# Eight fewer load transfers in a two-round attention and MLP decode kernel

## The chip, the cores and the metric

The kernel runs on one core of one Trainium2 chip. What counts is the device time of one execution in microseconds (us). Before the change three runs gave 711.56, 711.78 and 711.82 us, median 711.78.

The engines are named as the profile names them: PE (TensorE), DVE (VectorE), ACT (ScalarE), POOL (GpSimd) and SP (SyncE). SP computes nothing here; it issues the transfers (DMAs) from device memory into the core's own memory.

## The reference

Two layers are applied, and then applied again with the same weights: attention of one new token over a window of cached keys and values, and an MLP with ReLU. All of it is float32.

```python
x = x + attention(layernorm(x), k_cache, v_cache, wq, wo)   # 4 batches, 32 heads of 128, window 1024
x = x + relu(layernorm(x) @ w1) @ w2                        # 640 -> 1728 -> 640
x = x + attention(layernorm(x), k_cache, v_cache, wq, wo)
x = x + relu(layernorm(x) @ w1) @ w2
```

In the attention `q = x @ wq`, the scores of a head are q times the last 1024 keys, scaled and put through a softmax, the values are summed with these weights, and all heads together are multiplied with `wo`.

## The kernel before, in words

**Layout.** Everything that belongs to a head lies in one record of 9472 float32 columns on 128 partitions: 640 columns of `wq`, 4096 of keys, 4096 of values and 640 of `wo` (lines 47 to 48: `WQ, K, V, WO`, `REC`). A column here is 4 bytes on each of 128 partitions, 512 bytes. The records of all heads follow one another in `rec`, and `wm` holds the MLP's weights, 8640 columns of w1 and 8640 of w2. The data is larger than the core's memory and is read once in each round, except for what five heads keep.

**Places.** The tile `store` has a short front piece and five slots of a record each; `home(h, r)` (line 180) says which slot a head has. `ring` is a small buffer for the MLP's weights of round one, `kept` holds parts of head 26. Heads 27 to 31 are the last of round one and the first of round two, so their keys and values stay in place.

**The list of loads.** Lines 186 to 277 write the whole list of transfers, in order, into `items`. `load` (193) appends one; `run` (204) cuts a stretch of `rec` into the parts of its heads; `piece` (209) takes a part of one head; `group` (213) loads several heads in unequal transfers whose sizes `GROUPS` (82 to 85) gives; `ending` (219) loads the last three heads of a round in halves and, in round one, the six late `wo` parts (225 to 229), since these are used only after the last head. `W1_SLOT` (77) joins the five blocks of w1 of round two into transfers.

**What sets the order.** `pump` (279) issues the next item on SP when nothing that is still in use overlaps its destination (`live`); PE's steps call `done`, which frees places and pumps again. SP takes its instructions in order. A transfer also waits for the one eight places back in SP's list, whose semaphore it uses again. All other engines' instructions are recorded by one helper, so that in the profile of before nearly everything has line 102.

**Attention.** Heads are pipelined (513 to 538): in each step PE computes the scores of head n+1, the weighted values of head n, the query of head n+2, and then the transposed output of head n and its projection by `wo`. The softmax between them is on DVE and ACT. In the profile a PE row `misc<-xT,store` is a query (10 matmuls), `sc_ps<-store,qT` scores (16), `o_ps<-store,scratch` values (16), `t_ps<-rows,scratch` the transposed output, and `acc<-store,oTs` the projection. A row `acc<-kept,small` or `sc_ps<-kept,small` is one of the `busy` fillers (351), which compute nothing that is used.

**MLP.** `mlp` (460): the blocks of w1 in turn (`sc_ps<-ring,xT` or `sc_ps<-store,xT`), two transposes and the ReLU on DVE, then the tiles of w2 (`acc<-store,scratch`), two matmuls each. In round two w1 lies in the slot of head 22 and w2 in that of head 23, w2 in transfers of 22, 20, 8 and 4 tiles (3520, 3200, 1280 and 640 columns). A last copy on DVE and one transfer bring the result out.

Of the kernel before, what the change touches and what calls it, by code (L numbers as in the profile page):

```python
# [39 lines left out]
B, D, H, DH, W, FF = 4, 640, 32, 128, 1024, 1728  # L40
# [6 lines left out]
WQ, K, V, WO = 0, D, D + 4 * W, D + 8 * W  # L47
REC = 2 * D + 8 * W
# [28 lines left out]
W1_SLOT = [[0, 1], [2, 3], [4]]  # L77
# [5 lines left out]
LAST_FIVE = [REC + 4736, 2 * REC - 4736, REC, REC]  # L83
THREE = [REC + HALF, REC + HALF]
GROUPS = [{h: FIVE for h in range(0, 25, 5)}, {6: THREE, 9: FIVE, 14: FIVE, 19: LAST_FIVE}]
# [24 lines left out]
def decode_kernel(ctx: ExitStack, tc: tile.TileContext, xf, rec, wm, out):  # L110
# [82 lines left out]
    def load(src, lo, hi, buf, col, parts):  # L193
        items.append((src[:, lo:hi], buf, col, hi - lo, parts))
# [14 lines left out]
    def piece(r, h, lo, hi, buf="store", col=None):  # L209
        run(r, h * REC + lo, h * REC + hi, buf, home(h, r) + lo if col is None else col)  # L210
# [8 lines left out]
    def ending(r, hs, late):  # L219
        a, b, c = hs[-3:]  # L220
        end = WO if late else REC
        for h, lo, hi in ((a, 0, V), (b, 0, V), (a, V, end), (c, 0, V), (b, V, end), (c, V, WO if late else KEPT)):
            piece(r, h, lo, hi)
        if late:
            for h in hs[-1:] + hs[-LATE:-1]:
                if h == LAST - 1:
                    piece(r, h, WO, REC, "kept", WO - KEPT)
                else:
                    piece(r, h, WO, REC)
# [3 lines left out]
    for h in hs[:-3]:  # L233
        if h in GROUPS[0]:
            group(0, h, GROUPS[0][h])
        if h >= 25:
            piece(0, h, 0, KEPT if h == LAST - 1 else WO if h >= H - LATE else REC)
        if h == LAST - 1:
            piece(0, h, KEPT, WO, "kept", 0)
# [10 lines left out]
    for lo, hi, buf, col in IN_RING:  # L250
        piece(1, new[0], lo, hi, *place(buf, col))
    places = [("store", old[i] + lo, old[j] + hi) for i, lo, j, hi in (
        (0, 0, 0, K), (0, K + 1024, 0, K + VH), (0, K + VH + 1536, 0, V), (1, 0, 1, K), (1, K, 1, K + VH), (1, K + VH, 1, V),
# [25 lines left out]
    def pump():  # L279

        while items:
            src, buf, col, n, parts = items[0]
            if any(b == buf and x < col + n and col < y for b, x, y in live):
                return
            sp.dma_start(buffers[buf][:, col:col + n], src)
            live.append((buf, col, col + n))
            for key, lo, hi, c in parts:
                at.setdefault(key, []).append((lo, hi, buf, c))
            items.pop(0)
# [313 lines left out]
```

## Time and profile before

| what | value |
|---|---|
| median of 3 runs | 711.78 us |
| the profiled execution | 712.25 us |
| its span, first to last instruction of the program | 710.5 us |
| read from device memory | 301.34 MB, 424 GB/s over the span |
| time of the packets of SP's queue | 98.9% of 16 DMA engines' span |
| PE / DVE / ACT busy | 72% / 41% / 14% of the span |
| mean granted clock of PE | 0.803 |
| transfers | 87 from SP, 1 from ACT |

The profile has one execution. A row of an engine gives its start in us from the span's start, its length, the engine, the line, the operation with what it writes and reads, and in square brackets the idle time ahead of it with what ended it. Durations and the sum of the prediction are against the profiled execution; its span is 1.75 us shorter than its time, and its time 0.47 us above the median.

### The profile page before, as it was taken

Reading aid. Unit: us, or ns where it says so; the run is one execution under the profiler, and the core shown is the slowest. Engines: PE = TensorE matmul, PEld = TensorE weight load, DVE = VectorE, ACT = ScalarE, POOL = GpSimd, SP = SyncE. Lnnn points to the kernel's source line nnn. Section 1 sums busy time; section 2 is a strip of 40 time slices with the busy share of each in tenths; the row PEclk is TensorE's granted clock in tenths of the full one; section 3 lists DMA queues with packets and bytes.
Section 4 is the critical chain, followed back from the end, with each engine's and each line's share of the span. In section 5 each row is a group of like instructions: output and inputs, shape, how many; then the busy total and the mean of one; then the engine's idle time right before and its main releaser. Section 6 shows DMA issues by size and latency. Waiting matters only on the chain.

```text
span 710.5 us, 8480 instructions
## 1 busy us (share of the span) xinstructions
PE 513.0 (72%) x3722; PEld 214.0 (30%) x3722; DVE 293.3 (41%) x518; ACT 99.7 (14%) x210; POOL 1.1 (0%) x9
## 2 busy tenths in 40 slices
PE   0777586677584578869888999656584678686986
PEld 0332232232331223333323443222241232332322
DVE  3242353243342343435531775525162243453651
ACT  0110110011010110111120422101010011011110
POOL 0000000000000000000000000000000000000000
PEclk9977787677778776877999999968597677777989
DMA  9999999999999999999999999999999999999996
GB/s 398 439 416 447 425 435 443 414 439 450 418 435 441 424 437 421 423 439 423 430 398 403 412 426 433 445 435 437 431 435 426 438 436 430 432 432 416 433 425 281
DMA packets 12596, 301.96 MB, mean 425 GB/s; under 512 B 1408, under 2 KB 1552, under 8 KB 4624
## 3 DMA queue, kind: packets, MB, share of 16 engines
q1 hardware_dynamic: 12528, 301.42, 98.9%
q8 instruction: 29, 0.48, 0.2%
q14 instruction: 7, 0.06, 0.0%
q10 hardware_dynamic: 32, 0.01, 0.0%
HBM read 301.34 MB, written 0.08 MB: 424 GB/s over the span
## 4 chain that ended last, share of the span: by engine, by line
DMA 72%; PE 23%; DVE 4%; issue 1%; ACT 1%; ACTq 0%; SPq 0%; DVEq 0%
DMA store<-rec 65%; PE sc_ps L102 9%; PE o_ps L102 6%; DMA store<-wm 4%; PE acc L102 3%; PE misc L102 3%; DMA ring<-wm 2%; DVE scratch L102 2%; PE t_ps L102 1%; DVE o_ps L102 1%; ACT oTs L102 1%; DVE small L102 0%; DVE sc_ps L102 0%; ACT sc_ps L102 0%; ACTq L102 0%
## 5 line engine op out<-in xcount | busy, mean ns | idle before, releaser
L102 PE MATMUL sc_ps<-store,qT 128*32 128x512 f32 x1024 | 194.5, 849 | 35.7 <-DMA store<-rec 34.3
L102 PE MATMUL misc<-xT,store 128*128 128x4 f32 x620 | 95.6, 281 | 109.8 <-DMA store<-rec 109.8
L102 DVE TENSOR_REDUCE small<-sc_ps 128x1 f32<-128x1024 f32 x64 | 78.4, 1224 | 181.3 <-PE sc_ps L102 181.2
L102 PE MATMUL o_ps<-store,scratch 128*16 128x512 f32 x960 | 149.5, 701 | 1.7 <-DMA store<-rec 1.4
L102 PEld LDWEIGHTS misc<-xT,store 128*128 128x128 f32 x620 | 90.2, 227 | 166.6 <-DMA store<-rec 119.4
L102 ACT ACTIVATE sc_ps<-sc_ps,small 128x1024 f32<-128x1024 f32 x64 | 69.8, 1091 | 322.6 <-DVE small L102 322.6
L102 DVE STREAM_TRANSPOSE sc_ps<-sc_ps 128x1024 f32<-128x1024 f32 (+1 forms) x70 | 80.8, 1155 | 0.1
L102 PEld LDWEIGHTS sc_ps<-store,qT 128*32 128x32 f32 x1024 | 41.5, 139 | 112.4 <-issue 60.7
L102 PEld LDWEIGHTS o_ps<-store,scratch 128*16 128x16 f32 x960 | 33.8, 117 | 117.4 <-issue 107.8
L102 DVE TENSOR_TENSOR o_ps<-o_ps,of_block 128x512 f32<-128x512 f32 x62 | 43.3, 699 | 50.6 <-PE o_ps L102 50.6
L102 DVE TENSOR_TENSOR qT<-misc,rows 128x4 f32<-128x4 f32 x61 | 9.5, 155 | 112.9 <-PE misc L102 112.9
L102 PE MATMUL acc<-store,oTs 128*4 128x160 f32 x488 | 34.1, 363 | 17.0 <-ACT oTs L102 17.0
L102 DVE TENSOR_REDUCE scratch<-o_ps 128x128 f32<-128x512 f32 x62 | 42.9, 691 | 2.1
L102 ACT COPY oTs<-t_ps 128x4 f32<-128x4 f32 x59 | 9.6, 163 | 207.4 <-PE t_ps L102 207.4
L102 PE MATMUL t_ps<-rows,scratch 128*128 128x4 f32 x118 | 25.8, 289 | 11.3 <-DVE scratch L102 10.3
L102 PEld LDWEIGHTS t_ps<-rows,scratch 128*128 128x128 f32 x118 | 21.9, 231 | 17.4 <-DVE scratch L102 13.1
L102 DVE SCALAR_TENSOR_TENSOR scratch<-sc_ps,small,of_batch 128x128 f32<-128x128 f32 (+1 forms) x70 | 23.7, 339 | 3.5 <-PE o_ps L102 0.9
L102 PE MATMUL acc<-kept,small 128*1 128x328 f32 (+2 forms) x54 | 17.7, 433 | 0.0
L102 PEld LDWEIGHTS acc<-store,oTs 128*4 128x4 f32 x488 | 7.1, 84 | 22.5 <-ACT oTs L102 22.1
L102 ACT ACTIVATION_READ_ACCUMULATOR sc_ps<-sc_ps,small 128x1 f32 x64 | 12.3, 193 | 0.0
L102 DVE RECIPROCAL small<-small 128x1 f32<-128x1 f32 x64 | 9.8, 153 | 2.3 <-ACT sc_ps L102 2.3
L102 PE MATMUL acc<-store,scratch 128*4 128x160 f32 x146 | 6.1, 299 | 3.3 <-DMA store<-wm 3.2
(83 smaller groups left out, 99.8 us busy)
## 6 DMA issues: line engine op xcount, KB each, us to landing
store<-rec SPq DMA_DIRECT2D x14, 7872.0 KB, 27.3
store<-rec SPq DMA_DIRECT2D x7, 7936.0 KB, 29.9
store<-rec SPq DMA_DIRECT2D x4, 7104.0 KB, 30.8
store<-rec SPq DMA_DIRECT2D x11, 2368.0 KB, 36.5
store<-rec SPq DMA_DIRECT2D x3, 4736.0 KB, 25.7
store<-rec SPq DMA_DIRECT2D x2, 4416.0 KB, 29.1
store<-rec SPq DMA_DIRECT2D x3, 2048.0 KB, 40.7
store<-rec SPq DMA_DIRECT2D x1, 4160.0 KB, 21.6
```

The costliest lines, as they stand in the source:

```text
L102: r = build(*args, **kwargs)
```

## The change

Eight transfers go; every byte is still loaded, and to the same places.

- Round one's `wo` of heads 27 to 31 come as one transfer with five pieces of 640 columns per partition (`late_outputs`). For that the host writes these five `wo` into `rec` in the order of their slots, and the `wo` of head 26 now goes ahead of them.
- Head 25 and the front of head 26 are one transfer of 9472 + 6784 = 16256 columns.
- In round two, the two halves of 2048 columns between `K` and `V` of one place are one transfer of 4096.
- Round two's last group of five heads comes as 15744, 15872 and 15744 columns (`FIVE`) for 14208, 14208, 9472 and 9472 (`LAST_FIVE`).
- Round two's w1 comes as three and two blocks, where it came as two, two and one.

```diff
-W1_SLOT = [[0, 1], [2, 3], [4]]
+W1_SLOT = [[0, 1, 2], [3, 4]]
...
-LAST_FIVE = [REC + 4736, 2 * REC - 4736, REC, REC]
 THREE = [REC + HALF, REC + HALF]
-GROUPS = [{h: FIVE for h in range(0, 25, 5)}, {6: THREE, 9: FIVE, 14: FIVE, 19: LAST_FIVE}]
+GROUPS = [{h: FIVE for h in range(0, 25, 5)}, {6: THREE, 9: FIVE, 14: FIVE, 19: FIVE}]
...
     def load(src, lo, hi, buf, col, parts):
-        items.append((src[:, lo:hi], buf, col, hi - lo, parts))
+        items.append((src[:, lo:hi], buffers[buf][:, col:col + hi - lo], [(buf, col, col + hi - lo)], parts))
+
+    def late_outputs():
+
+        slots = [(home(h, 0) + WO, home(h, 0) + REC) for h in range(LAST, H)]
+        src = rec.rearrange("p (h c) -> p h c", c=REC)[:, LAST:, WO:]
+        dst = store[:, FIRST:].rearrange("p (h c) -> p h c", c=REC)[:, :, WO:]
+        items.append((src, dst, [("store", a, b) for a, b in slots],
+                      [(("rec", 0, LAST + i), WO, REC, a) for i, (a, _) in enumerate(slots)]))
...
         if late:
-            for h in hs[-1:] + hs[-LATE:-1]:
-                if h == LAST - 1:
-                    piece(r, h, WO, REC, "kept", WO - KEPT)
-                else:
-                    piece(r, h, WO, REC)
+            piece(r, LAST - 1, WO, REC, "kept", WO - KEPT)
+            late_outputs()
...
-        if h >= 25:
-            piece(0, h, 0, KEPT if h == LAST - 1 else WO if h >= H - LATE else REC)
-        if h == LAST - 1:
-            piece(0, h, KEPT, WO, "kept", 0)
+        if h == LAST - 2:
+            run(0, h * REC, h * REC + REC + KEPT, "store", home(h, 0))
+            piece(0, LAST - 1, KEPT, WO, "kept", 0)
+        elif h >= LAST:
+            piece(0, h, 0, WO)
...
-        (0, 0, 0, K), (0, K + 1024, 0, K + VH), (0, K + VH + 1536, 0, V), (1, 0, 1, K), (1, K, 1, K + VH), (1, K + VH, 1, V),
+        (0, 0, 0, K), (0, K + 1024, 0, K + VH), (0, K + VH + 1536, 0, V), (1, 0, 1, K), (1, K, 1, V),
...
-            src, buf, col, n, parts = items[0]
-            if any(b == buf and x < col + n and col < y for b, x, y in live):
+            src, dst, spans, parts = items[0]
+            if any(b == buf and x < hi and lo < y for b, x, y in live for buf, lo, hi in spans):
                 return
-            sp.dma_start(buffers[buf][:, col:col + n], src)
-            live.append((buf, col, col + n))
+            sp.dma_start(dst, src)
+            live.extend(spans)
...
-    rec[:, :, WO:] = np.asarray(A_wo).reshape(H, DH, D)
+    wo = np.asarray(A_wo).reshape(H, DH, D)
+    rec[:, :, WO:] = wo
+    rec[H - NS:, :, WO:] = wo[[next(h for h in range(H - NS, H) if h % NS == i) for i in range(NS)]]
```

The instructions of PE, DVE, ACT and POOL stand in the same order as before; only SP's list differs. Late in round one SP had, for head 25, the front of head 26, and what follows (the first row ends the group of heads 20 to 24):

```order
L102 DMA store<-rec 128x15744
L102 DMA store<-rec 128x9472
L102 DMA store<-rec 128x6784
L102 DMA kept<-rec 128x2048
L102 DMA store<-rec 128x8832 x2
```

and has now:

```order
L101 DMA store<-rec 128x15744
L101 DMA store<-rec 128x16256
L101 DMA kept<-rec 128x2048
L101 DMA store<-rec 128x8832 x2
L101 DMA store<-rec 128x4736 x2
```

The transfers of 9472 and 6784 columns have become one of 16256, ahead of the same rows.

At the end of round one's loads, from the last halves of heads 30 and 31 to the first weights of the MLP, SP had:

```order
L102 DMA store<-rec 128x4736
L102 DMA store<-rec 128x4096 x2
L102 DMA store<-rec 128x640
L102 DMA kept<-rec 128x640
L102 DMA store<-rec 128x640 x4
L102 DMA ring<-wm 128x1728 x2
```

and has now:

```order
L101 DMA store<-rec 128x4736
L101 DMA store<-rec 128x4096 x2
L101 DMA kept<-rec 128x640
L101 DMA store<-rec 128x5x640
L101 DMA ring<-wm 128x1728 x2
```

The part for `kept` moved to the front, and the five for `store` are one row behind it.

In round two, from the last group of five heads (19 to 23) through the halves of heads 24 to 26 to the MLP's weights, SP had:

```order
L102 DMA store<-rec 128x15744
L102 DMA store<-rec 128x14208 x2
L102 DMA store<-rec 128x9472 x2
L102 DMA store<-rec 128x4736 x5
L102 DMA store<-rec 128x2048
L102 DMA store<-wm 128x3456 x2
L102 DMA store<-wm 128x1728
L102 DMA store<-wm 128x3520
L102 DMA store<-wm 128x3200
```

and has now:

```order
L101 DMA store<-rec 128x15744 x2
L101 DMA store<-rec 128x15872
L101 DMA store<-rec 128x15744
L101 DMA store<-rec 128x4736 x5
L101 DMA store<-rec 128x2048
L101 DMA store<-wm 128x5184
L101 DMA store<-wm 128x3456
L101 DMA store<-wm 128x3520
L101 DMA store<-wm 128x3200
```

The first row of 15744 belongs to the group before. The four transfers of heads 19 to 23 are three, and the last of them now reaches from the middle of head 22 to the end of head 23; w1 has one transfer less.

## Rows read from the trace of the kernel before

**Rows 1.** The page: SP's DMA queue, and the chain that ended last.

```profile
q1 hardware_dynamic: 12528, 301.42, 98.9%
...
DMA 72%; PE 23%; DVE 4%; issue 1%; ACT 1%; ACTq 0%; SPq 0%; DVEq 0%
```

**Rows 2.** SP's issues in time, four of round one: start, length.

```profile
344.44 0.33 SPq L102 DMA_DIRECT2D store<-rec  x1
...
350.04 0.33 SPq L102 DMA_DIRECT2D store<-rec  x1
...
359.75 0.33 SPq L102 DMA_DIRECT2D ring<-wm  x1
...
360.53 0.33 SPq L102 DMA_DIRECT2D ring<-wm  x1
```

**Rows 3.** Two stretches: busy time of each engine, PE's clock, DMA share, GB/s.

```profile
360.00:400.00 40.00, 35.15 (x342) 14.10 (x334) 13.82 (x40) 8.51 (x15) 0.00 (x0) 0.96 1.00 396
400.00:420.00 20.00, 18.55 (x175) 8.60 (x178) 13.86 (x22) 4.75 (x11) 0.00 (x0) 1.00 1.02 433
```

**Rows 4.** DMA issues by size: count, KB each, median us from issue to landing.

```profile
store<-rec SPq DMA_DIRECT2D x11, 2368.0 KB, 36.5
...
store<-rec SPq DMA_DIRECT2D x1, 3392.0 KB, 29.2
store<-rec SPq DMA_DIRECT2D x3, 1024.0 KB, 8.1
...
store<-wm SPq DMA_DIRECT2D x1, 1280.0 KB, 6.5
...
out<-scratch SPq DMA_DIRECT2D x1, 80.0 KB, 1.6
```

**Rows 5.** The chain that ended last, in order of time: start, length, what.

```profile
203.84 24.60 DMA store<-rec
...
673.03 31.83 DMA store<-wm
...
704.90 2.83 PE acc L102 x68
```

**Rows 6.** PE in time, end of round one's attention and its MLP.

```profile
363.87 0.74 PE L102 MATMUL acc<-store,oTs 128*4 128x160 f32 x16
...
372.29 1.25 PE L102 MATMUL sc_ps<-store,xT 128*4 128x432 f32 x9 [0.80 <-DMA store<-wm]
```

**Rows 7.** PE in time, round two, behind the last transfer of two groups.

```profile
542.94 1.07 PE L102 MATMUL sc_ps<-store,qT 128*32 128x512 f32 x3 [8.49 <-DMA store<-rec]
...
553.33 2.76 PE L102 MATMUL o_ps<-store,scratch 128*16 128x512 f32 x16
...
599.26 0.96 PE L102 MATMUL sc_ps<-store,qT 128*32 128x512 f32 x3 [2.87 <-DMA store<-rec]
...
609.61 1.93 PE L102 MATMUL o_ps<-store,scratch 128*16 128x512 f32 x16
```

**Rows 8.** PE in time, round two, from head 23's query to the last fillers.

```profile
656.22 1.28 PE L102 MATMUL misc<-xT,store 128*128 128x4 f32 x10 [3.60 <-DMA store<-rec]
...
663.28 1.28 PE L102 MATMUL misc<-xT,store 128*128 128x4 f32 x10
...
678.60 1.28 PE L102 MATMUL misc<-xT,store 128*128 128x4 f32 x10 [0.75 <-DMA store<-rec]
...
684.30 3.61 PE L102 MATMUL o_ps<-store,scratch 128*16 128x512 f32 x16
...
694.12 1.09 PE L102 MATMUL sc_ps<-store,xT 128*4 128x432 f32 x8
...
698.78 1.15 PE L102 MATMUL acc<-kept,small 128*1 128x328 f32 x4
```

**Rows 9.** Two stretches at the end, columns as in rows 3.

```profile
660.86:681.34 20.48, 18.13 (x158) 7.88 (x154) 12.29 (x21) 3.94 (x8) 0.00 (x0) 1.00 1.00 428
681.34:688.16 6.82, 6.39 (x38) 1.48 (x34) 4.14 (x8) 1.37 (x3) 0.00 (x0) 0.50 1.01 429
```

More of the change, by code (lines that the diff above doesn't have):

```diff
@@ L281, in pump @@
         while items:
-            src, buf, col, n, parts = items[0]
-            if any(b == buf and x < col + n and col < y for b, x, y in live):
+            src, dst, spans, parts = items[0]
+            if any(b == buf and x < hi and lo < y for b, x, y in live for buf, lo, hi in spans):
                 return
-            sp.dma_start(buffers[buf][:, col:col + n], src)
-            live.append((buf, col, col + n))
+            sp.dma_start(dst, src)
+            live.extend(spans)
             for key, lo, hi, c in parts:
-                at.setdefault(key, []).append((lo, hi, buf, c))
+                at.setdefault(key, []).append((lo, hi, spans[0][0], c))
             items.pop(0)
```

## The prediction

> **What bounds the kernel now.** I read the page's DMA and chain sections first [rows 1]. One queue carries nearly everything and its packets fill 98.9% of the time of all 16 DMA engines; the chain that ended last is 72% DMA. So the sum of bytes, and whatever each transfer costs beside them, sets the time. Then the queue of SP, where a late `wo` transfer of 640 columns (a column is 4 bytes on 128 partitions, 512 B) is issued the moment an older transfer lands, so that its issue times are landing times [rows 2]. 4736 columns land 5.60 us after their predecessor (344.44 to 350.04), 640 columns 0.78 us after theirs (359.75 to 360.53). That is (5.60 - 0.78) / 4096 = 1.177 ns a column and 0.78 - 640 x 0.001177 = 0.03 us that a transfer costs besides its data.
>
> Last I read the end of the span on PE. The chain waits for the transfer of 3200 columns until 704.86, and from 704.90 PE works 2.83 us through the last tiles of w2, then DVE copies [rows 5]. The transfers behind it are the same 1280 and 640 columns in both kernels. The end is thus the landing of the 3200 columns plus about 5.6 us, as long as PE is ready for it.
>
> **What goes.** SP issues 79 transfers for 87 (ACT's one stays). Four go with the five late `wo`, and one each with: head 25 with the front of head 26, two value-and-key pieces of round two (2048 + 2048), round two's last five heads (three transfers for four), and w1 (two for three). Bytes are the same. By the landings, 8 x 0.03 = 0.24 us. From above: the stretch with most short transfers moves 396 GB/s, the one behind it 433 [rows 3]. If all of that loss, 40 x (1 - 396/433) = 3.4 us over some 24 transfers (landings from 360.5 to 398.9), were a cost by transfer, it would be 0.14 us each, 1.15 us for eight. From below: no row has a transfer with five pieces a partition; the nearest are the single 640-column ones, whose pieces are as long, and whose 0.78 us already holds their packets. So the saving could be nothing. I take 0.2 us, near the direct row.
>
> **Which waits grow.** A joined transfer is issued when the last of its places is free. What covers that is the queue ahead of it: the time from issue to landing, less its own data. A lone transfer on an empty queue (the output) lands 1.6 us after issue, 0.2 of it data, so more than 1.4 us of queue hides an issue completely [rows 4].
> - Head 25 with 26: the 6784 columns of before land 29.2 us after issue with 8.0 of data. 11.1 of the rest is head 25, now in the same transfer; 10 us of queue stay.
> - 2048 + 2048: the median of the three transfers of 1024 KB is the second of this pair, 8.1 us. Less 4.8 of joint data, 3.3 us stay.
> - Groups of five heads as 15744, 15872 and 15744: the shortest issue to landing of one is 24.60 us [rows 5], less 18.5 of data, 6.1 us. The last group now has the pattern of the others.
> - w1: its places come free when head 22's values are done, about 668 below, and its data starts at 692.7 - 6.1 = 686.6 (below); 18 us.
> - Five pieces: a usual SP issue is 0.33 us [rows 2]. Even five of them, 1.7 us, stand behind 10 us of queue.
> So no joined issue leaves the queue dry.
>
> **Which landings come later.** Joining gives up early landings, and that costs where PE is not waiting anyway.
> - Late `wo`. Before, the six land 0.78 us apart from 360.5 to 364.4; now the kept one first and five together at about 364.2. PE projects heads 27 and 28 at 363.87 [rows 6], so this slips by 0.4 us or so. Behind it the MLP begins on weights that have landed, and PE waits 0.80 us for the next at 372.29: covered. The issues that depend on it have at least 3.5 us of queue (1280 KB: 6.5 us less 3.0 of data) [rows 4], 3.0 after the slip, over the 1.4 needed.
> - Head 25 lands 8.0 us later, with the front of head 26. PE's backlog lasts until it catches up with heads 27 to 31, which land at DMA's pace; the halves of heads of 2368 KB that are issued meanwhile are of a kind that lands 36.5 us after its issue (median of eleven in both rounds) [rows 4], 31 of it queue. Nothing.
> - w1: the first joined part lands 10176 columns ahead of the 3200 ones, 704.65 - 12.0 = 692.7, and PE starts on w1 at 694.12 [rows 8]. Nothing.
> - Round two's last group. Before, heads 22 and 23 land separately, PE takes up head 23's query at 656.22 and head 24's at 663.28 [rows 8], 7.1 us later. Now half of head 22's keys, its values and all of head 23 land together at 656.0. This is the pattern of the other groups [rows 7]: PE starts on the rest of the scores at 599.26 and ends the values, ready for the query after next, at 609.61 + 1.93 = 611.54, 12.3 us later. So head 24's query slips by 12.3 - 7.1 = 5.2, less 0.2 for the earlier landing, to 668.3.
>
> That backlog is the one term that can reach the end. Heads 24 to 26 then take the same steps as before at the full clock (1.00 from 660.86 to 681.34 [rows 9]). At 678.60 PE had waited 0.75 us for the last query, so 4.25 us remain. Behind it the granted clock stood at 0.50, the lower level of 1.2 GHz, from 681.34 to 688.16 [rows 9], after that wait and a short query. A PE that comes late has no such wait. At the full level the values of head 25 need 1.93 (as at 609.61) for 3.61 us [rows 7, 8], and 4.25 - 1.7 = 2.55 us remain. The fillers ahead of w2 end at 698.78 + 1.15 = 699.93, so PE is ready at 702.5. The first 22 tiles are 44 matmuls, 1.83 us at the 2.83 for 68 [rows 5], and must be done when the 3200 columns land at 704.65: up to 702.8 nothing is lost. That leaves 0.3 us to spare, little, but on the side of no loss.
>
> **Sum.** Only DMA's saving is left: -0.2 us on a span of 710.5 and an execution of 712.25 us. That execution is 0.47 above the median of the runs, 711.78, so the forecast for the median is 711.6. From about 0.2% (1.4 us) on a difference can be told from none; this is no change.
>
> **Rivals.**
> 1. PE comes too late for w2. It decides from 702.8. If the clock falls at the last query as before, the 4.25 us stay, w2 begins at 704.2, and PE ends 704.2 + 1.83 + 2.83 - 707.73 = 1.1 us later: 712.9. If the group also starts as slowly as at 542.94, ready at 553.33 + 2.76 = 556.09, 13.15 us later [rows 7], 0.9 more: 713.8. I put the case at 713.3. For it: the spare time is 0.3 us and rests on a clock that these rows do not fix. Against: PE was at the full level through all of the stretch that it now reaches without a pause. The Trainium skill (DMA: Bandwidth & Descriptors, "Why a DMA increments its semaphore by 16 and not by 1") says that only the full count means that all data has landed; by it head 22 gets nothing from the joined transfer early, the trace agrees (the scores resume only at 599.26), and this rival cannot be softened by early rows.
> 2. Transfers cost the 0.14 us of the bound from above: -1.15 us, 710.6. For it the low rate in [rows 3]; against it the 0.03 of [rows 2].
> 3. A transfer holds the engines for the 1.4 us that the lone output needs beside its data [rows 4]: eight of them, 11 us, 700.6. Against it, landings 0.78 us apart with 0.75 of data [rows 2]. The Trainium skill (the same page, "Anatomy of one DMA") gives a fixed cost near 2.0 us a transfer, and its "Rules for kernel authors" ask to coalesce; taken as engine time that would be 16 us. The trace disagrees: it lies beside other transfers.
> 4. The MLP's short transfers start late: the 0.4 us slip is three or more, the 3.5 us of queue runs out, and 1 to 3 us are lost: 713.5.
>
> **How the numbers follow.** Forecast 0.63, rivals 0.22, 0.10, 0.01 and 0.04. Below 710.4 lie rival 3 and a fifth of rival 2: faster 0.03. Above 713.2 lie half of rival 1 and a part of rival 4: slower 0.12. Same 0.85. The range goes from rival 2's 710.6 to 713.2, with about 0.06 left out below and 0.12 above.
>
> **What would show it.** Right: DMA busy throughout; the 3200 columns land 0.1 to 0.4 us earlier; PE idle for some us ahead of 656 and then busy without a pause past 680; a short wait for the 3200 columns still there near 704.5. Wrong: no wait of PE for w2, and the last tiles begin after 705 (rival 1); 396 GB/s from 360 to 400 well up (rival 2); gaps between packets there (rival 4).

## The result: slower, by about 1.5 us

The changed kernel takes **713.32 us** (median of 19 runs, 712.06 to 715.51), the kernel before **711.78 us** (median of 19 runs in the same comparison, 710.93 to 713.58). The ratio is **1.0021, 95% interval 1.0012 to 1.0031**: slower, though by little, and 0.1 us beyond the upper end of the predicted range. The profiled execution took 713.34 us with a span of 711.6, where before it was 712.25 and 710.5.

### The profile after

The page of the changed kernel: packets of the whole span, SP's queue, and the chain that ended last, which answer to [rows 1].

```profile
DMA packets 11956, 301.96 MB, mean 424 GB/s; under 512 B 1280, under 2 KB 1424, under 8 KB 4368
...
q1 hardware_dynamic: 11888, 301.42, 98.9%
...
DMA 63%; PE 29%; DVE 5%; ACT 1%; issue 1%; another core or an unknown queue 1%; ACTq 0%; SPq 0%; DVEq 0%
```

The same bytes go in 640 packets fewer (12528 on this queue before, 11888 now), at the same share of the 16 engines. So DMA still carries the kernel, and joining bought nothing that could be seen: had the transfers' own cost held the queue back, the mean rate should have risen, and it went from 425 to 424 GB/s.

Windows of the changed kernel, with the columns of [rows 3] (the last three are PE's granted clock, DMA's share, GB/s): the stretch with the short transfers, and the one behind it.

```profile
360.00:400.00 40.00, 34.94 (x341) 13.91 (x334) 13.44 (x37) 8.45 (x15) 0.00 (x0) 0.96 0.99 386
400.00:420.00 20.00, 18.54 (x168) 8.33 (x170) 13.87 (x25) 4.80 (x12) 0.00 (x0) 1.00 1.01 430
```

386 GB/s for 396: over 40 us that is 0.4 MB, or 0.9 us at the 430 of the row below. The execution's span is 1.1 us longer. Here, then, nearly all of it is lost, in the end of round one's attention and in its MLP.

PE's timeline of the changed kernel, for the end of round one's attention and the MLP's first blocks (start, length, and at the end the idle time before and what ended it).

```profile
364.49 0.73 PE L101 MATMUL acc<-store,oTs 128*4 128x160 f32 x16 [0.44 <-DMA store<-rec]
...
367.67 1.04 PE L101 MATMUL sc_ps<-ring,xT 128*4 128x432 f32 x8
...
372.33 1.25 PE L101 MATMUL sc_ps<-store,xT 128*4 128x432 f32 x9 [0.23 <-DMA store<-wm]
...
374.75 0.91 PE L101 MATMUL sc_ps<-ring,xT 128*4 128x432 f32 x8 [0.81 <-DMA ring<-wm]
```

The same place in the kernel before (rows not shown ahead; the values of head 31 first).

```profile
359.87 3.06 PE L102 MATMUL sc_ps<-store,scratch 128*16 128x512 f32 x16 [2.45 <-DVE scratch L102]
...
367.06 1.04 PE L102 MATMUL sc_ps<-ring,xT 128*4 128x432 f32 x8
...
374.35 0.91 PE L102 MATMUL sc_ps<-ring,xT 128*4 128x432 f32 x8 [0.45 <-DMA ring<-wm]
```

The projection of heads 27 and 28 now waits for a transfer, 0.62 us later than the 363.87 of [rows 6], and the MLP's first block starts 0.61 us later. The transfer that PE next waits for lands when it did (372.33, for 372.29 in [rows 6]), but the one behind it, the first that reuses the ring, lands 0.4 us later. SP's timeline says why. The first columns of the ring are free when PE's first block of the MLP has read them; only then is their reload issued. Before:

```profile
368.18 3.13 SPq L102 DMA_DIRECT2D ring<-wm  x3
```

and in the changed kernel:

```profile
368.79 3.13 SPq L101 DMA_DIRECT2D ring<-wm  x3
```

The last transfer ahead of the reload is the one of 2160 columns (1080 KB) that was issued at 364.30; on the page of before it is

```profile
store<-wm SPq DMA_DIRECT2D x1, 1080.0 KB, 7.9
```

so it lands at 372.2 (372.24 by the trace). Thus 4.06 us of queue stood before this reload, and now 3.5. I call this number the queue ahead of the reload; it is the number that decides, as the experiments show.

At the end, PE's timeline of the changed kernel, answering to [rows 7, 8].

```profile
657.20 1.07 PE L101 MATMUL sc_ps<-store,qT 128*32 128x512 f32 x3 [6.86 <-DMA store<-rec]
...
669.48 1.28 PE L101 MATMUL misc<-xT,store 128*128 128x4 f32 x10
...
703.80 1.15 PE L101 MATMUL acc<-kept,small 128*1 128x328 f32 x4
704.75 4.00 PE L101 MATMUL acc<-store,scratch 128*4 128x160 f32 x112
```

and its clock where [rows 9] had 1.00:

```profile
660.86:681.34 20.48, 18.52 (x146) 8.07 (x144) 11.57 (x20) 3.68 (x9) 0.00 (x0) 0.83 1.00 429
```

The last group of five behaves as forecast: one long wait, then a backlog, with head 24's query 12.3 us behind the first scores. PE reaches w2 at 704.75 and runs its 112 matmuls without a wait, where before 68 of them stood behind the landing of the 3200 columns [rows 5]. So PE, not a landing, now ends the chain, which looks like rival 1. But PE was hardly late: the 3200 columns, issued at 674.88 and 30.9 us under way,

```profile
store<-wm SPq DMA_DIRECT2D x1, 1600.0 KB, 30.9
```

landed at 705.80, 0.94 us later than before (704.86), and PE ended w2 2.95 us behind that landing, where before it needed 2.83. So of the 1.1 us by which this span is longer, 0.94 are a later landing and 0.1 PE. The experiments e1 and e4 below say the same.

### The profile page after: what moved, and what is told of

Same layout as the page of the kernel before. It is cut to its first block, busy times and chain, and to the rows that moved or that the text cites. A ratio compares the mean times of both kernels' runs of the same rounds, so it can differ in the third digit from the quotient of the medians.

```text
span 711.6 us, 8466 instructions
## 1 busy us (share of the span) xinstructions
PE 497.6 (70%) x3722; PEld 209.8 (29%) x3722; DVE 293.0 (41%) x518; ACT 99.6 (14%) x210; POOL 1.1 (0%) x9
## 2 busy tenths in 40 slices
DMA packets 11956, 301.96 MB, mean 424 GB/s; under 512 B 1280, under 2 KB 1424, under 8 KB 4368
## 3 DMA queue, kind: packets, MB, share of 16 engines
q1 hardware_dynamic: 11888, 301.42, 98.9%
## 4 chain that ended last, share of the span: by engine, by line
DMA 63%; PE 29%; DVE 5%; ACT 1%; issue 1%; another core or an unknown queue 1%; ACTq 0%; SPq 0%; DVEq 0%
DMA store<-rec 61%; PE sc_ps L101 12%; PE o_ps L101 8%; PE acc L101 5%; PE misc L101 3%; DVE scratch L101 2%; DVE o_ps L101 2%; DMA ring<-wm 2%; PE t_ps L101 2%; ACT oTs L101 1%; DVE small L101 0%; ACT sc_ps L101 0%; DVE sc_ps L101 0%; ACTq L101 0%
## 5 line engine op out<-in xcount | busy, mean ns | idle before, releaser
L101 PE MATMUL sc_ps<-store,qT 128*32 128x512 f32 x1024 | 190.0, 829 | 45.6 <-DMA store<-rec 44.3
L101 PE MATMUL misc<-xT,store 128*128 128x4 f32 x620 | 93.8, 278 | 115.6 <-DMA store<-rec 115.6
L101 PE MATMUL o_ps<-store,scratch 128*16 128x512 f32 x960 | 142.8, 664 | 3.8 <-DVE small L101 1.4
L101 PEld LDWEIGHTS misc<-xT,store 128*128 128x128 f32 x620 | 88.4, 223 | 171.0 <-DMA store<-rec 123.5
L101 PEld LDWEIGHTS o_ps<-store,scratch 128*16 128x16 f32 x960 | 32.0, 112 | 111.9 <-issue 100.8
L101 ACT ACTIVATION_READ_ACCUMULATOR sc_ps<-sc_ps,small 128x1 f32 x64 | 12.3, 193 | 0.0
```

The source lines that it names most:

```text
L101: r = build(*args, **kwargs)
```

## The experiments

Four theories are named in the expectations:
- **T**: the last group of five makes PE late for w2 (rival 1).
- **W** (in some texts M): the five late `wo` come in one landing, PE starts the MLP late, the ring's reload is issued late, and DMA runs dry (rival 4).
- **P**: a transfer of several pieces a partition disturbs the DMA engines by itself.
- **C**: PE's wait for the five pieces makes the granted clock fall, and PE's slowness costs, whatever the DMA does.

Each was timed in five rounds against the kernel before on the same chip, whose median was 711.83 to 712.13 us in those comparisons. The last three columns are of its profiled execution: the reload's issue, and GB/s in the windows 364 to 372 and 364 to 400 us. Behind 400 us all of them move 431 to 433 GB/s until 680, and counted in bytes no profiled execution regains or adds more than 0.3 us between 400 and 680. What an execution gains or loses behind 680 the table doesn't show; e9 and e16 below lost 1 to 2 us there.

| | median us (runs) | ratio, 95% interval | reload | 364:372 | 364:400 |
|---|---|---|---|---|---|
| before | 711.78 (19) | | 368.18 | 385 | 392 |
| changed | 713.32 (19) | 1.0021 (1.0012 to 1.0031) | 368.79 | 368 | 382 |
| e1 | 715.54 (6) | 1.0045 (1.0032 to 1.0057) | 370.13 | 320 | 371 |
| e2 | 713.01 (11) | 1.0017 (1.0008 to 1.0025) | 368.73 | 369 | 381 |
| e3 | 712.30 (11) | 1.0003 (0.9994 to 1.0012) | 367.62 | 397 | 390 |
| e4 | 711.71 (11) | 1.0000 (0.9991 to 1.0009) | 367.65 | 397 | 401 |
| e5 | 714.49 (5) | 1.0038 (1.0025 to 1.0051) | 370.58 | 326 | 370 |
| e6 | 712.60 (11) | 1.0011 (1.0002 to 1.0020) | 368.72 | 382 | 393 |
| e7 | 711.70 (12) | 0.9999 (0.9990 to 1.0009) | 367.69 | 394 | 396 |
| e8 | 712.38 (12) | 1.0018 (1.0004 to 1.0033) | 370.92 | 313 | 357 |
| e9 | 713.25 (12) | 1.0015 (1.0003 to 1.0027) | 368.54 | 378 | 380 |
| e10 | 711.95 (12) | 1.0000 (0.9988 to 1.0012) | 367.54 | 397 | 403 |
| e11 | 713.03 (12) | 1.0016 (1.0007 to 1.0026) | 370.35 | 324 | 365 |
| e12 | 713.92 (12) | 1.0022 (1.0013 to 1.0032) | 369.88 | 336 | 367 |
| e13 | 712.38 (11) | 1.0005 (0.9996 to 1.0014) | 368.11 | 390 | 390 |
| e14 | 712.65 (11) | 0.9998 (0.9982 to 1.0013) | 367.56 | 393 | 400 |
| e15 | 713.64 (11) | 1.0017 (1.0007 to 1.0027) | 367.73 | 396 | 387 |
| e16 | 712.28 (11) | 1.0008 (0.9999 to 1.0016) | 367.60 | 397 | 394 |
| e17 | 713.15 (11) | 1.0013 (1.0004 to 1.0022) | 370.18 | 324 | 386 |
| e18 | 715.24 (6) | 1.0053 (1.0041 to 1.0065) | 373.10 | 307 | 353 |

### Which part of the change costs (e1 to e5)

**e1**: the changed kernel, with the last group of five in four transfers again.

```diff
...
-GROUPS = [..., {6: THREE, 9: FIVE, 14: FIVE, 19: FIVE}]
+GROUPS = [..., {6: THREE, 9: FIVE, 14: FIVE, 19: LAST_FIVE}]
```

> The changed kernel, but heads 19 to 23 of round two come in four transfers again (14208, 14208, 9472, 9472). Theory T (PE comes late to the last MLP because heads 22 and 23 land together): the loss goes, 711.5 to 712.0 us (ratio to before 0.9995 to 1.0005), PE waits for w2 twice again, near 701 and 705. Theory M (the joined late wo let the MLP of round one start 0.6 us later and its short loads lose 0.7 to 1 us of DMA time there): 712.3 to 712.9 (1.0008 to 1.0015), the last load lands 0.7 us or more after that of before although PE waits for w2.

**e2**: the changed kernel, with six single late `wo` again.

```diff
-            piece(r, LAST - 1, WO, REC, "kept", WO - KEPT)
-            late_outputs()
+            for h in hs[-1:] + hs[-LATE:-1]:
+                ...
+                    piece(r, h, WO, REC)
...
```

> The changed kernel, but round one's late wo are six transfers again, in the old order; the other joins stay. Theory T: no change from the changed kernel, 712.8 to 713.5 us (1.0015 to 1.0025), no wait of PE for w2. Theory M: 711.9 to 712.6 (1.0003 to 1.0012), the load issued first in the second round of ring buffers (1728 columns) is issued at 368.2 us again and the DMA from 370 to 400 us runs as before.

**e3**: both of these edits. 

> Both undone: six late wo and four transfers for heads 19 to 23; heads 25 and 26, the 4096 columns of round two and w1 stay joined. T and M together, or either: 711.4 to 712.0 us (0.9995 to 1.0003). If one of the three joins that stay costs something, 712.3 or more.

e1 was slower than the changed kernel, not faster: T falls as the cause. Neither theory had its 715.54 us. e3, which keeps heads 25 and 26, the 4096 columns and w1 joined, can't be told from before, though its 712.30 lies a little above what its text expected. e2's 713.01 lies in T's range, not in M's: taking the late `wo` apart alone gave back little. Its profiled execution shows why, there at least. The values of head 31, which took 3.06 us before,

```profile
360.03 3.54 PE L101 MATMUL sc_ps<-store,scratch 128*16 128x512 f32 x16 [2.43 <-DVE scratch L101]
```

ran nearly all at half clock (0.50 from 360.17 to 363.58), and with single late `wo` and no wait for them the reload still came at 368.73, as late as in the changed kernel, with the same 369 and 381 GB/s. So two parts were left, and each was made alone, in the kernel before.

**e4**: `19: LAST_FIVE` becomes `19: FIVE`, and nothing else.

> The kernel of before with only the last group of round two in three transfers (15744, 15872, 15744). Theory T: the whole loss is here, 712.8 to 713.5 us (1.0015 to 1.0025), w2's matmuls run without a wait and begin after 703.7. Theory M: 711.6 to 712.2 (1.000 to 1.0006); PE comes late to w2 by less than it can make up.

**e5**: only the late `wo` are joined, with the code for it.

```diff
-            for h in hs[-1:] + hs[-LATE:-1]:
-                ...
+            piece(r, LAST - 1, WO, REC, "kept", WO - KEPT)
+            late_outputs()
```

> The kernel of before with only round one's late wo joined (kept one first, then five pieces in one transfer); all other loads as before. Theory M (PE waits for the five pieces, begins the MLP of round one some 0.6 us later, issues the ring's next loads later, and the DMA engines run dry there): 712.6 to 713.8 us (1.0012 to 1.0028), gaps of the DMA engines between 364 and 400 us above the 0.8 us of before. Theory T (the last group of five heads): 711.5 to 712.0 (0.9995 to 1.0004).

e5 alone gives 714.49 us, 1.0038, more than its text expected (713.8 at most); e4 gives no loss. Yet in e4 PE is as late for w2 as forecast (its timeline):

```profile
702.20 4.40 PE L102 MATMUL acc<-store,scratch 128*4 128x160 f32 x112
```

It takes up w2 at 702.2 without a wait, inside the 702.8 that the prediction had as its deadline, and no time is lost. In e5 PE waits for the five pieces:

```profile
364.85 0.73 PE L102 MATMUL acc<-store,oTs 128*4 128x160 f32 x16 [1.98 <-DMA store<-rec]
...
369.19 0.60 PE L102 MATMUL sc_ps<-ring,xT 128*4 128x432 f32 x3
```

and SP's first reload of the ring is

```profile
370.58 3.13 SPq L102 DMA_DIRECT2D ring<-wm  x3
```

2.4 us later than before. The wait of 1.98 us is not all of it. The granted clock of e5 falls behind that wait to 0.50, 1.2 GHz:

```profile
365.95:369.36 3.41, 3.41 (x33) 1.60 (x29) 1.05 (x6) 1.42 (x2) 0.00 (x0) 0.50 0.94 392
```

e1 shows the same, 2.01 us of wait and then 0.50 from 365.54:

```profile
364.40 0.73 PE L102 MATMUL acc<-store,oTs 128*4 128x160 f32 x16 [2.01 <-DMA store<-rec]
```

```profile
365.54:368.95 3.41, 3.41 (x33) 1.63 (x29) 1.12 (x6) 1.39 (x2) 0.00 (x0) 0.50 0.94 394
```

The profiled executions of before and of the changed kernel had such a low stretch earlier, before's from 360.49, the changed kernel's from 360.41 (the window 360 to 364 shows 0.57 in both). PE was then late for the late `wo` by itself, and the single landing cost only 0.6 us. In e1 and e5, whose clock is full at 360 us, it costs 2 us of wait, and half speed behind it.

### Lateness without the join (e6, e7), and another order (e8)

**e6** and **e7**: the kernel before, with one and with two fillers ahead of the late projections.

```diff
+        if late > 2:
+            busy()
```

> The kernel of before, all its loads unchanged, with one more filler (two matmuls of 328 columns, 0.6 us) on PE ahead of the late projections of round one. Theory M: the same loss as the joined late wo, 712.4 to 713.8 us (1.001 to 1.0028). Theory P (the transfer of five pieces itself disturbs the DMA engines): 711.6 to 712.1 (0.9998 to 1.0004).

> As the run before it, with two fillers (1.2 us). Theory M: more than with one, 713.0 to 714.8 us (1.0017 to 1.004), longer gaps of the DMA engines from 364 to 400 us. Theory P: 711.6 to 712.3.

e6 slipped as W says and lost 0.1%, though the interval reaches down to 0.02%; its profiled execution moves 382 GB/s up to 372 us but 393 up to 400, no less than before, so the trace doesn't tie that 0.1% to the reload. e7 missed (713.0 to 714.8 us by W, 711.70 measured): its execution had the clock full from 360 to 372 us, PE started on the ring's first weights at 366.73, hardly behind their landing at 366.59 in spite of two fillers, the reload was issued at 367.69, and nothing was lost. That speaks against "later work costs" and for "a later reload costs".

**e8**: the changed kernel, with the five pieces ahead of the kept head and the projections in another order, heads 27 to 31 first.

```diff
-            piece(r, LAST - 1, WO, REC, "kept", WO - KEPT)
             late_outputs()
+            piece(r, LAST - 1, WO, REC, "kept", WO - KEPT)
...
-        for i in range(late - 3) if late > 2 else (0,):
+        for i in (1, 2, 3) if late > 2 else (0,):
...
```

> The changed kernel with all its 80 transfers, but the five pieces are loaded ahead of the part for kept, and PE projects heads 27, 28, 29, then 30, 31 and last 26, so that it does not wait for the five. Theory M: the loss goes or nearly, 711.4 to 712.5 us (0.9994 to 1.001). Theory P or T: as the changed kernel, 712.8 to 713.8 (1.0014 to 1.0028).

The five land sooner, but in the profiled execution PE still waits 1.61 us and its clock falls; the reload comes at 370.92. The median is in M's range, but the runs fall in two groups: eight of 711.7 to 712.6 us and four of 713.8 to 716.5, of which the profiled one (715.17) is one. The ratio is 1.0018, with an interval that holds the changed kernel's 1.0021: a gain isn't shown.

### Clock or reload (e9 to e12)

**e9**: the changed kernel with two fillers in the wait for the five. **e10** and **e11**: the kernel before, and the changed one, with three more fillers behind head 30's values. **e12**: e11 with four fillers in the wait.

```diff
+            if late > 2 and i == 0:
+                busy()
+                busy()
```

```diff
-        values(r, hs[-2], 0, (0, 1))
+        values(r, hs[-2], 0, (0, 1 if r else 4))
```

> The changed kernel with two fillers (1.2 us at the full clock) on PE between the late projection of head 26 and those of heads 27 and 28, where PE waits for the five pieces. Theory C (PE's wait for the five pieces, 0.4 to 2.0 us, lets the granted clock fall to 0.50 at the start of round one's MLP; PE then releases the ring 2 us later and the DMA engines run dry): the clock stays at 1.00 from 364 to 372 us in most executions, 711.6 to 712.6 us (0.9998 to 1.001). Theory P (the transfer of five pieces itself disturbs the DMA engines): as the changed kernel, 712.8 to 713.8.

> The kernel of before with three more fillers (1.8 us) behind the values of head 30 in round one, where PE waits 2.45 us for DVE, so that the clock is at 1.00 when the values of head 31 start. Nothing waits for the late wo here. Theory C: same or a little faster, 710.8 to 711.9 us (0.9986 to 1.0001), clock 1.00 from 360 to 372. Theory P: 711.6 to 712.0.

> The changed kernel with the same three fillers. PE ends the values of head 31 earlier, at 361.7, in every execution, and so waits 2 us for the five pieces in every one. Theory C: slower than the changed kernel though PE is faster, 714 to 716 us (1.003 to 1.006), clock 0.50 from some 365 to 369, the first load of the ring's second round issued near 370.6. Theory P, or a slip of PE alone: as the changed kernel or better, 712.0 to 713.4.

> As the run before it, with four more fillers (2.4 us) in the wait for the five pieces. Theory C: the clock stays at 1.00, PE begins the MLP near 366.8, the ring's load is issued near 368, and most of the loss goes: 711.4 to 712.6 us (0.9995 to 1.001). Theory P: 712.0 to 713.8.

e9 and e12 kept the clock at 1.00 from 360 to 372 us and were no faster for it (1.0015, 1.0022): C alone falls. Their reload was still late (368.54, 369.88). e10 (711.95) equals before. e11 missed its number, 714 to 716 forecast and 713.03 measured, though its reload was as late as it said. e9, e10 and e11 lie in the ranges of P, which e13 and e14 decide, and e12's 713.92 just above P's. In e9's profiled execution, the slowest of its twelve, PE reached w2 only at 706.32 and ended it 3.8 us behind the landing of the 3200 columns (706.51), where before it needed 2.83: there rival 1's lateness cost 1 us.

### One landing or two (e13, e14)

**e14**: the changed kernel, with the five late `wo` in two transfers, three pieces and two, so that heads 27 and 28 land with the first. **e13**: the same in e1.

```diff
+        for a, b in ((2, 5), (0, 2)):
...
+            src = rec.rearrange("p (h c) -> p h c", c=REC)[:, LAST + a:LAST + b, WO:]
+            dst = store[:, FIRST:].rearrange("p (h c) -> p h c", c=REC)[:, a:b, WO:]
...
```

> The slowest kernel so far (changed kernel with heads 19 to 23 in four transfers, 715.5 us) with one thing else: round one's five late wo come in two transfers, three pieces (heads 27 to 29) and two (30, 31), so that PE can project heads 27 and 28 near 362.8 us instead of 364.4. Theory W (PE's wait for the joined late wo makes the first reload of the ring late, and the DMA engines run dry): 711.6 to 712.8 us (0.9997 to 1.0013), reload issued before 368.3. Theory P (transfers with several pieces disturb the DMA engines): 713.5 to 716.

> The changed kernel with the late wo as three and two pieces. Theory W: the part of the loss that the late wo make goes, 711.7 to 713.0 us (0.9998 to 1.0016; the upper end if the last group of five heads with the other joins costs what the run with six late wo showed). Theory P: as the changed kernel or worse, 713.0 to 714.0.

e13 against e1, 1.0005 for 1.0045, and e14 against the changed kernel, 0.9998 for 1.0021, differ in this one cut. Both came out in W's range. A transfer of three pieces a partition is still there, so P falls. e13's difference is clear; e14's is less so, for its interval (0.9982 to 1.0013) reaches that of the changed kernel, and its median is 0.52 us above that of before in the same comparison. In e14 PE has its pieces two us sooner than in e5, and the reload is early:

```profile
362.58 0.73 PE L101 MATMUL acc<-store,oTs 128*4 128x160 f32 x16 [0.44 <-DMA store<-rec]
```

```profile
367.56 3.55 SPq L101 DMA_DIRECT2D ring<-wm  x3
```

### Two that left something open (e15, e16)

**e15**: the changed kernel, with six late `wo` and heads 25 and 26 apart; the last group of five, w1 and the 4096 columns stay joined.

```diff
-        if h == LAST - 2:
-            run(0, h * REC, h * REC + REC + KEPT, "store", home(h, 0))
-        ...
+        if h >= 25:
+            piece(0, h, 0, KEPT if h == LAST - 1 else WO if h >= H - LATE else REC)
...
```

> The run with six late wo (1.0017) with heads 25 and 26 apart again; left of the change are the last group of five in three transfers, w1 in two and the 4096 columns in one. If the joined heads 25 and 26 made that run slow: 711.5 to 712.2 us (0.9995 to 1.0005). If w1 or the 4096 columns with the group of five did, or PE's late arrival at w2: 712.6 to 713.4 (1.001 to 1.002).

1.0017, as e2, and 713.64 us is above what its text expected of either case (713.4 at most). Its profiled execution has an early reload (367.73), so the reload doesn't explain it; e2's has a late one. Why these two kernels are slow in most runs isn't shown.

**e16**: the kernel before, with the place of the first weights released one block later in the program.

```diff
-            done(("w", r), k * FF, k * FF + FF)
+            if r or k:
+                done(("w", r), (k - 1 if k == 1 else k) * FF, k * FF + FF)
```

> The kernel of before, PE's work and all transfers unchanged, but in round one's MLP the place of w1's first block is given free only with the second block, so that the first reload of the ring is issued some 1.5 to 2 us later (near 370). No late wo is joined, PE does not wait for them. Theory W: that alone makes the loss, 713.0 to 715.5 us (1.0017 to 1.005), gaps of the DMA engines between 364 and 402 us of 1.8 us or more (0.8 before). If the lateness of the issue does not matter: 711.6 to 712.2.

The issue did not move (367.60): it waits for PE's last read of the place, wherever the release is written. So e16 is in effect the kernel before once more, and its 1.0008 shows how far apart two such medians may lie. Its profiled execution, 714.34 us, shows a loss that no window ahead of 680 has. PE waited 2.39 us for the first transfer of w2, the granted clock was 0.50 from 702.52 to 709.34, and the last 68 matmuls took 4.67 us where before they took 2.83 [rows 5]:

```profile
705.12 4.67 PE L102 MATMUL acc<-store,scratch 128*4 128x160 f32 x68 [1.33 <-DMA store<-wm]
```

The 3200 columns had landed at 705.08, only 0.2 us later than before. So about 2 us of this execution are PE's clock at the very end, not DMA.

### The reload alone (e17, e18)

In the kernel before, one filler of the MLP reads the first weights instead of kept columns, so that the reload waits for that filler. In **e17** it is the filler behind the second block, in **e18** the one at the end of the third (before, that one stood in the middle of the third), two matmuls behind a landing. Transfers are as before, and so is PE's work, but for the place of one filler in e18.

```diff
...
-                    busy()
-            done(("w", r), k * FF, k * FF + FF)
+                    busy(src=ring if k * FF + FQ * (j + 1) == 3456 else kept)
+            if r or k >= 1:
+                done(("w", r), (0 if k == 1 else k) * FF, k * FF + FF)
```

> The kernel before, all transfers as they were. One filler of round one's MLP (128x328, its result goes into the same unused columns) reads the first weights in the ring instead of kept columns, and the release of those columns is written behind it; so the reload of that part of the ring waits for this filler, and PE's instructions are otherwise the same in number, shape and order. The reload's issue should move from 368.18 to 369.8 to 370.3 us, the queue ahead of it from 4.06 to about 2.2 us. Theory W (the loss of the change is nothing but this late reload: the 16 DMA engines are then partly dry around 371 us and all later loads land later): last load 0.8 to 1.8 us later than in the profile before, median 712.7 to 713.7. Rival C (the loss comes from the clock of PE or from the shape of the joined transfers, the late reload only goes along with it): no change, 711.6 to 712.2, since 2.2 us of queue are more than the 1.4 us that a lone transfer needs.

> As e17, but the filler that reads the first weights stands two matmuls into the third block, which wait for a landing at 372.2 us: the reload is issued at about 372.8 us, some 0.5 us after the transfer ahead of it has landed, so that the queue is surely empty for a while. Theory W: all 16 engines idle from about 372.3 to 373.7 us, most of them longer, 3 to 4 us lost at once, perhaps more where the next reloads come late in their turn: median 714.8 to 718. Rival C: what an empty queue costs is only the gap that can be seen between the landing and the first packets, 1.5 us: 713.2 or below.

Both came out where W had them: 713.15 us (712.7 to 713.7 forecast) and 715.24 (714.8 to 718). e17's median alone proves little, since its interval (1.0004 to 1.0022) overlaps e16's; the trace and e18, whose 1.0053 is clear of everything, carry the argument. PE's MLP starts at 366.99 in e17, as before (367.06); the reload's issue is moved to 370.18, and the two issues behind it follow at 370.60 and 371.09 (369.74 and 370.99 before):

```profile
370.18 1.28 SPq L102 DMA_DIRECT2D ring<-wm  x3
```

This is what it does to the DMA engines. Windows of 1 us, the kernel before (the last two columns are DMA's share and GB/s):

```profile
369.00:370.00 1.00, 1.00 (x11) 0.34 (x5) 0.00 (x0) 0.00 (x0) 0.00 (x0) 1.00 0.93 302
370.00:371.00 1.00, 1.00 (x6) 0.26 (x3) 0.00 (x0) 0.00 (x0) 0.00 (x0) 1.00 0.93 368
371.00:372.00 1.00, 0.49 (x2) 0.00 (x0) 0.00 (x0) 0.00 (x0) 0.00 (x0) 1.00 0.96 403
372.00:373.00 1.00, 0.71 (x8) 0.21 (x10) 0.00 (x0) 0.00 (x0) 0.00 (x0) 1.00 1.07 372
```

e17:

```profile
369.00:370.00 1.00, 1.00 (x12) 0.34 (x6) 0.00 (x0) 0.00 (x0) 0.00 (x0) 1.00 0.62 259
370.00:371.00 1.00, 1.00 (x7) 0.24 (x3) 0.00 (x0) 0.00 (x0) 0.00 (x0) 1.00 0.33 138
371.00:372.00 1.00, 0.43 (x2) 0.00 (x0) 0.00 (x0) 0.00 (x0) 0.00 (x0) 1.00 0.89 185
372.00:373.00 1.00, 0.75 (x10) 0.23 (x12) 0.00 (x0) 0.00 (x0) 0.00 (x0) 1.00 0.96 380
```

e18, whose reload and two next issues come at 373.10, 373.52 and 374.00:

```profile
367.00:368.00 1.00, 1.00 (x12) 0.38 (x4) 0.00 (x0) 0.18 (x1) 0.00 (x0) 1.00 1.08 453
368.00:369.00 1.00, 0.79 (x10) 0.19 (x9) 0.18 (x1) 0.09 (x1) 0.00 (x0) 1.00 0.79 328
369.00:370.00 1.00, 1.00 (x13) 0.27 (x5) 0.00 (x0) 0.00 (x0) 0.00 (x0) 1.00 0.58 245
370.00:371.00 1.00, 0.68 (x4) 0.00 (x0) 0.00 (x0) 0.00 (x0) 0.00 (x0) 1.00 0.37 156
371.00:372.00 1.00, 0.00 (x0) 0.00 (x0) 0.00 (x0) 0.00 (x0) 0.00 (x0) 1.00 0.08 35
372.00:373.00 1.00, 0.85 (x10) 0.46 (x12) 0.00 (x0) 0.00 (x0) 0.00 (x0) 1.00 0.00 0
373.00:374.00 1.00, 1.00 (x9) 0.17 (x2) 0.00 (x0) 0.00 (x0) 0.00 (x0) 1.00 0.00 0
374.00:375.00 1.00, 0.15 (x1) 0.00 (x0) 0.00 (x0) 0.00 (x0) 0.00 (x0) 1.00 0.91 166
```

e18 is the clearest. The transfer ahead lands at 372.1 (PE takes it up at 372.15), so by landings the queue is busy until then. But the share of the engines falls from 368 on: 0.79, 0.58, 0.37, 0.08. The 16 engines don't end their parts of the queue together. The trace has 16 increments of the semaphore for the last transfer ahead, which I read as one for each engine's part: in e18 they come from 368.75 to 372.10, 3.35 us apart, in the kernel before from 368.86 to 372.24. The landing tells only of the last. A reload issued 2 us ahead of that landing (e17) is late for most of them. And behind e18's issue at 373.10 nothing moves before 374.04, 0.94 us. So a reload that is to find no engine idle needs some 3.35 + 0.94 = 4.3 us of queue, an estimate from these two numbers.

## Why the prediction was wrong

**What bounds the kernel**: held in the main. DMA carries the span in every profile, and what the changed kernel and e18 lose they lose as DMA time. From the GB/s of 364 to 400, at 432 GB/s: (392 - 353) x 36 / 432 = 3.3 us for e18, whose span is 3.1 longer, and (392 - 382) x 36 / 432 = 0.8 us for the changed kernel, whose span is 1.1 longer. Not all executions are like that: e16's lost about 2 us to PE's clock in w2 and e9's 1 us to a late PE, behind the last long landing. Such ends are part of the scatter of the medians.

**What goes**: held as far as can be told. Eight transfers fewer are worth nothing that a ratio shows (e3 keeps three of the four single joins, e4 the fourth, and e14 has seven of the eight; 1.0003, 1.0000 and 0.9998). That leaves no room for rival 3. For rival 2 the medians are too coarse, for e14's interval would hold its 0.14 us a transfer; but its sign, a rate well up from 360 to 400, is absent: from 364 to 400 us e14, with seven transfers fewer and an early reload, moves 400 GB/s, and e10, with all of them and as early a reload, 403.

**Which waits grow**: this step failed. The prediction took "more than 1.4 us of queue hides an issue completely" from a lone output, and found 3.5 us of queue, 3.0 behind the slip: covered. So it put the term of the late `wo` at nothing. (Its 3.5 was read from the 1280 KB transfer that is issued at 373.93; the reload that decided, issued at 368.18, isn't in its sum.) The lone output shows what an issue needs when it meets an empty queue. It doesn't show when the queue becomes empty, and landings don't either. By the runs, the stretch from 364 to 372 us moves 393 to 397 GB/s in the seven kernels whose reload is issued by 367.8, 368 to 390 where it comes from 368.1 to 368.8, and 307 to 336 where it comes at 369.9 or later. With the landing ahead at 372.2, some 4.4 us of queue are needed, not 1.4, close to the 4.3 estimated from e18. The changed kernel's 3.5 is already on the slope, and so is before's 4.06 a little.

**Which landings come later**: "slips by 0.4 us or so" is 0.6 in the profiled execution, and in the profiles of e1 and e5 the reload is 2.0 and 2.4 us late. It was read from one execution in which PE happened to be at half clock from 360.49, and so to be late for the late `wo` anyway. Where PE is on time, as in e1 and e5, the one landing makes it wait until 364.4 to 364.9. The Trainium skill (DMA: Bandwidth & Descriptors, "Why a DMA increments its semaphore by 16 and not by 1") says that only the full count tells that the data is there; the traces agree, heads 27 and 28 begin only when all five pieces have landed. The prediction reckoned with that here too ("five together at about 364.2"); what it didn't ask is when PE would be ready for them in an execution at full clock.

**The last group of five**: held. Head 24's query came 12.3 us behind the first scores, as worked out, and in e4 PE was ready for w2 at 702.2 (702.5 predicted). In the changed kernel it was 704.75, 1.2 us of it from the later landing (657.20 for 656.0) and the rest beside a clock of 0.83 where 1.00 was assumed. It cost about 0.1 us, since the 3200 columns came later too. e1 takes this lateness away and gains nothing.

**The rivals**: rival 4 is what happened, and it had 4 chances in 100. That its price fits (713.5; 713.32 measured) is luck: its condition was a slip of "three or more" us, from the wrong 1.4 us, and 0.6 already loses something. Rival 1's sign, no wait for w2, is in the profile too; it cost 0.1 us there and nothing in e4, and 1 us in the profiled execution of e9.

Rival 3's sentence on the Trainium skill (DMA: Bandwidth & Descriptors, "Anatomy of one DMA") leaves out that this section is on transfers issued by gpsimd. SP issues those here, and the rival doesn't rest on that sentence.

**How much is accounted for.** The late reload alone is worth 1.2 us by medians (e17, 713.15 for the 711.97 beside it; its interval is 0.3 to 1.6). e5 has it as late and loses 2.7: there PE is late for the whole MLP, and the next issues slip as well (376.85 for 375.32 in SP's timeline). e17 moves 403 GB/s from 372 to 400, e5 383. In the changed kernel's profiled execution the late reload accounts for the loss: from 364 to 400 us it is 0.8 us behind, and at the end its 3200 columns land 0.94 us later, nearly all of the 1.1 by which its span is longer. That its other executions, whose median difference is 1.5, are a mixture of this and of e5's kind is likely and not shown, as each kernel has one profile. What stays open: why e2 and e15, with single late `wo`, still run 0.17% slower, nearly as much as the whole change, although neither the group of five (e4) nor the joins (e3) does alone; and why e1 is slower than the changed kernel though it does less to PE. No version beat the kernel before: e14, the change with the late `wo` in two landings, can't be told from it.

## What to carry to other kernels

Before joining transfers, ask who takes up the first piece, and whether he is on time in an execution at full clock: one landing for five pieces is a wait for the last of them. The queue ahead of an issue, read from landings, has to be longer than the spread of the 16 engines, which the DMA share in windows of 1 us shows, plus the time from an issue to its first data; here that was about 4.4 us, three times what the lone transfer suggested. Where the queue was kept full, as here, one, three and seven transfers fewer (e4, e3, e14) gave no gain that could be measured. And one profile shows one place of PE's stretch at half clock; whether a consumer is on time has to be asked for an execution at full clock too.

## What the hardware showed unexpectedly

- Engines of one queue end far apart: DMA's share falls from 1.08 (367 to 368 us in e18) over 0.79, 0.58 and 0.37 to 0.08, all ahead of the landing at 372.1. The 16 increments of the transfer that lands there are 3.35 us apart. Behind the empty queue the next transfer's are 0.55 us apart (376.93 to 377.48).
- A wait of PE of about 2 us ahead of 364.4 to 364.9 was followed, 1.1 us behind its end, by 3.41 us at a granted clock of 0.50 (e1, e5): a short wait cost PE twice. At the end of e16 a wait of 2.39 us was followed by 6.82 us at 0.50, and the last matmuls took 4.67 us for 2.83.
- Five pieces a partition in one transfer cost DMA nothing: the kept piece and the five of the changed kernel have landed by 364.45, the six of before by 364.44.
